# P V as four 64x64 products side by side instead of one product against a block diagonal, in a fused attention and SwiGLU kernel

## The chip, the cores and the metric

The kernel runs on one core of a Trainium2 chip. TensorE (PE) multiplies matrices: a 128x128 block of weights is loaded, and up to 512 columns of the other operand stream through it into a bank of PSUM, the accumulator memory (eight banks, each 128 partitions by 512 fp32). VectorE (DVE), ScalarE (ACT) and GpSimd (POOL) do elementwise work, and only the first two of these three take part in emptying PSUM here; SyncE (SP) issues DMAs. Each engine works through its own queue in order and waits for others by semaphores. The metric is the device time of one execution in microseconds (us), smaller is better.

## The reference

Linformer attention and then a SwiGLU feed-forward block, for 8 batches, 8 heads, 1024 positions, head size 64, 512 model columns, 1536 hidden columns:

```python
k_proj = einsum('ks,bhsd->bhkd', E, k)            # E, F: 64 x 1024
v_proj = einsum('ks,bhsd->bhkd', F, v)            # 64 x 64 per head
attn = softmax(q @ k_proj.T / sqrt(64))           # 1024 x 64 per head
attn_out = attn @ v_proj                          # "P V", 1024 x 64 per head
x = attn_out, heads side by side                  # 8192 x 512
out = (silu(x @ w_gate) * (x @ w_val)) @ w_out    # 8192 x 512
```

In P V both the contraction (64 projected positions) and the output (64 columns of a head) are half as wide as TensorE's array.

## The kernel before

The output rows are done in 16 chunks of 512, two for each batch. The main loop runs over 192 iterations t = 12 c + f: chunk c, block f of 128 hidden columns. Each iteration has four products for the gate (`f_g`, bank tag gps, line 462), four for the value (`f_v`, bank tag vps, line 462), and one or two steps of the down projection of the chunk before (`f_m`, line 564, seven steps for each of two row pairs, in banks y and z, also called yps). ACT takes a tanh of the gate (line 474); DVE multiplies (lines 481, 486). The down projection forms half its products from sums of quarters, hs, made by POOL and DVE (line 547), and its results leave through ACT, DVE and POOL (lines 581 to 600).

The attention of the next batch is spread between these products. The order is written out by hand: every iteration has two slots, 2t after `f_g` and 2t+1 at its end, `put(slot, function, ...)` places a step in a slot, and `place(b)` does so for batch b, with slots counted from s0 = 48 (b - 1). Within a slot loads come first, then steps in the order of their `put`. Nothing is rearranged afterwards. The steps of a batch b are:

- loads of k, v and q from POOL's queue (`load_k`, `load_v`, `load_q`);
- `u_KV`: the k and v projections of all heads, in pairs of products of 64 array columns each; ACT copies k out to ks, DVE copies v out into the block diagonal BDV;
- `u_KT`: k transposed by TensorE, and copied by DVE in four pieces into the block diagonal BD (lines 275, 276);
- `u_TD`, `u_AD`: q and the normalized scores transposed by DMAs from SP's queue, into qTd and AT (bufs=2 each);
- `u_S`, `u_R`, `u_N`: scores of four heads for 256 rows (four products, exp on ACT), sums and reciprocals on DVE, the multiply on POOL into AAd; eight of each for a batch;
- `u_PV`: P V. A pair of heads has its two 64x64 blocks of v on the diagonal of a 128x128 weight block, BDV, whose other two blocks are zero; one product of 512 columns gives both heads of the pair (line 410), and a copy on ACT (line 150) takes it from a bank to xT, which `f_g` and `f_v` read. A chunk has four such products, in four slots.

The pool ps_a has two banks ("a"); g and v have two, y and z one each. Batch 0 and batch 1 have their own arrangements; batch 0's P V runs through `u_PV`, `u_PV2` and `u_PV1`.

Of the kernel before, what the change touches and what calls it, by code (L numbers as in the profile page):

```python
# [16 lines left out]
H = 8  # L17
S = 1024
D = 64
# [19 lines left out]
def kernel(  # L39
# [38 lines left out]
    ident_bf = const.tile([P, P], BF16, name="ident_bf")  # L78
    ident_fp = fw.tile([P, P], FP32, name="ident_fp", tag="th")
    BD = [const.tile([P, H, P], BF16, name=f"BD{i}") for i in range(2)]  # L80
    BDV = [const.tile([P, NPAIR, P], BF16, name=f"BDV{i}") for i in range(2)]
    ks = [const.tile([P, H, D], BF16, name=f"ks{i}") for i in range(2)]
    ksp = [const.tile([P, NPAIR, D], BF16, name=f"ksp{i}") for i in range(2)]
    ET = const.tile([P, NJ, KP], BF16, name="ET")
# [57 lines left out]
    def bank(where, shape, dt, name):  # L142
        if where == "a" and ring["wide"]:
            where = "aaz"[ring["n"] % 3]
            ring["n"] += 1
        pool, tag = banks[where]
        return pool.tile(shape, dt, name=name, tag=tag)
# [4 lines left out]
    def u_KV(b, what="kv", hs=(0, H), at="a"):  # L152

        key = (b, what)
        if key not in kvp:
            kvp[key] = bank(at, [P, H, D], FP32, "kvp")
        t = kvp[key]
        h0, h1 = hs
        todo = [x for x in (("k", 0, ET, kb), ("v", 64, FT, vb)) if x[0] in what]
        for j in range(NJ):  # L160
            for _, lo, w, src in todo:
                nc.tensor.matmul(  # L162
                    out=t[lo : lo + 64, h0:h1].rearrange("p h d -> p (h d)"),
                    lhsT=w[:, j, :],
                    rhs=src[b][:, h0:h1, j, :],
                    start=(j == 0),
                    stop=(j == NJ - 1),
                )
        if "k" in what:
            nc.scalar.copy(out=ks[b % 2][0:64, h0:h1], in_=t[0:64, h0:h1])  # L170
        if "v" in what:
            tv = t[64:128].rearrange("p (a c) d -> p a c d", c=2)
            ps = slice(h0 // 2, h1 // 2)
            nc.vector.tensor_copy(out=BDV[b % 2][0:64, ps, 0:64], in_=tv[:, ps, 0, :])
            nc.vector.tensor_copy(out=BDV[b % 2][64:128, ps, 64:128], in_=tv[:, ps, 1, :])
        if h1 == H:
            kvp.pop(key)

# [15 lines left out]

    def u_V1(b, at="a"):

        t = bank(at, [P, NPAIR, D], FP32, "kvp")
        src = vb[b][:].rearrange("p (a c) j d -> p a c j d", c=2)
        for j in range(NJ):
            for c in range(2):  # L200
                nc.tensor.matmul(
                    out=t[64 * c : 64 * c + 64],
                    lhsT=FT[:, j, :],
                    rhs=src[:, :, c, j, :],
                    start=(j == 0),
                    stop=(j == NJ - 1),
                )
        for c in range(2):
            rows = slice(64 * c, 64 * c + 64)
            nc.vector.tensor_copy(out=BDV[b % 2][rows, :, rows], in_=t[rows])  # L210

    def u_V0(p0, p1, at):

        t = bank(at, [P, p1 - p0, P], FP32, "kvp")
        nc.tensor.matmul(
            out=t[:].rearrange("p a d -> p (a d)"),
            lhsT=zeros[:, 0:P], rhs=zeros[:, 0 : (p1 - p0) * P],
            start=True, stop=False,
        )
        src = vb[0][:].rearrange("p (a c) j d -> p a c j d", c=2)  # L220
        for j in range(NJ):
            for c in range(2):
                nc.tensor.matmul(
                    out=t[64 * c : 64 * c + 64, :, 64 * c : 64 * c + 64],
                    lhsT=FT[:, j, :],
                    rhs=src[:, p0:p1, c, j, :],
                    start=False,
                    stop=(j == NJ - 1),
                )
        nc.scalar.copy(out=BDV[0][:, p0:p1, :], in_=t[:])  # L230

    def u_V0w(p0, p1, at):

        t = bank(at, [P, p1 - p0, 2, D], FP32, "kvp")
        for j in range(NJ):
            nc.tensor.matmul(
                out=t[64:P].rearrange("p a c d -> p (a c) d"),
                lhsT=FT[:, j, :],
                rhs=vb[0][:, 2 * p0 : 2 * p1, j, :],
                start=(j == 0),  # L240
                stop=(j == NJ - 1),
            )
        for c in range(2):
            rows = slice(64 * c, 64 * c + 64)
            nc.scalar.copy(out=BDV[0][rows, p0:p1, rows], in_=t[64:P, :, c, :])

    def turn_ksp(t, b, g):
        nc.tensor.matmul(
# [95 lines left out]
    def u_S(b, u, at="a"):  # L344
        ch, w = divmod(u, 4)
        g, i = divmod(w, 2)
        ps = bank(at, [P, 4, P], FP32, "sc")
        if (b, ch) in BY_DMA:
            t = qT[b, ch, "d"][:].rearrange("p (h i) t -> p i h t", i=2)[:, i, 4 * g : 4 * g + 4]
        else:  # L350
            t = qT.pop((b, u))
        for n in range(4):
            nc.tensor.matmul(  # L353
                out=ps[:, n, :], lhsT=t[:, n, :], rhs=BD[b % 2][:, 4 * g + n, :], start=True, stop=True
            )
        e = aw.tile([P, 4, 2, KP], FP32, name="ee", tag="ee", bufs=4)
        nc.scalar.activation(  # L357
            out=e[:].rearrange("p h j k -> p (h j k)"),
            in_=ps[:].rearrange("p a k -> p (a k)"),
            func=AF.Exp,  # L360
            scale=scale,
        )
        ee[b, u] = e
# [42 lines left out]
    def u_PV(b, ch, pr, eng=nc.scalar):  # L406
        if (b, ch) not in xT:
            xT[b, ch] = x_pool.tile([P, NPAIR, CW], BF16, name="xT", tag=f"xT{ch}")
        ps = bank("a", [P, CW], FP32, "pv")
        nc.tensor.matmul(  # L410
            out=ps[:].rearrange("p (j t) -> p j t", t=P),
            lhsT=BDV[b % 2][:, pr, :],
            rhs=AT[b, ch][:, :, pr, :],
            start=True,
            stop=True,
        )
        copy(eng, xT[b, ch][:, pr, :], ps[:])

    def u_PV2(b, ch, g, i, eng):

        if (b, ch) not in xT:
            xT[b, ch] = x_pool.tile([P, NPAIR, CW], BF16, name="xT", tag=f"xT{ch}")
        ps = bank("a", [P, 2, CW // 2], FP32, "pv")
        for n in range(2):
            nc.tensor.matmul(
                out=ps[:, n].rearrange("p (j t) -> p j t", t=P),
                lhsT=BDV[b % 2][:, 2 * g + n, :],
                rhs=AT[b, ch][:, 2 * i : 2 * i + 2, 2 * g + n, :],
                start=True,
                stop=True,  # L430
            )
        copy(eng, xT[b, ch][:, 2 * g : 2 * g + 2, 256 * i : 256 * (i + 1)], ps[:])

    def u_PV1(b, ch, pr, i, eng):

        ps = bank("a", [P, CW // 2], FP32, "pv")
        nc.tensor.matmul(
            out=ps[:].rearrange("p (j t) -> p j t", t=P),
            lhsT=BDV[b % 2][:, pr, :],
            rhs=AT[b, ch][:, 2 * i : 2 * i + 2, pr, :],  # L440
            start=True,
            stop=True,
        )
        copy(eng, xT[b, ch][:, pr, 256 * i : 256 * (i + 1)], ps[:])
# [211 lines left out]
    def put(s, fn, *a):  # L656
        slots[s].append((fn, a))

    def place(b):
        s0 = 48 * (b - 1)  # L660
        if b == 1:
            put(22, u_TD, 1, 0)
            put(29, u_K1, 1)
            put(32, u_KT, 1)
            put(40, u_V1, 1)
            sa = (35, 36, 37, 38, 41, 42, 43, 44)
            put(41, u_AD, 1, 0)
            put(30, u_TD, 1, 1)
            put(47, u_AD, 1, 1)
            sp = (44, 45, 46, 46, 66, 67, 68, 69)  # L670
        else:
            put(s0 + (10 if b == 2 else 0), u_KV, b)
            put(s0 + (13 if b == 2 else 3), u_KT, b)
            o = 17 if b == 2 else 6
            put(s0 + (9 if b == 2 else -6), u_TD, b, 0)
            put(s0 + (11 if b == 2 else -4), u_TD, b, 1)
            sa = [s0 + o + 3 * j for j in range(NJ)]
            put(sa[3] + 4, u_AD, b, 0)
            put(sa[7] + 4, u_AD, b, 1)
            sp = [s0 + i for i in ((41, 43, 45, 46) if b == 2 else (39, 41, 43, 45)) + (57, 59, 61, 63)]  # L680
        for j in range(NJ):
            put(sa[j], u_S, b, j)
            put(sa[j] + 1, u_R, b, j)
            put(sa[j] + 1, u_N, b, j)
        for i in range(8):
            put(sp[i], u_PV, b, i // 4, i % 4)

    def run_slot(s):
        for fn, a in slots.pop(s, ()):
# [2 lines left out]
    with tc.manual_schedule():  # L692
# [17 lines left out]
        make_identity(nc, ident_fp[:])  # L710
        make_identity(nc, ident_bf[:])
        nc.vector.memset(ks[0][64:P], 0.0)
        nc.vector.memset(BDV[0][:, 0:2], 0.0)

        def turn(which, at, halves=(0, 1), eng=nc.scalar):
            for half in halves:
# [79 lines left out]
        f_mm(0, 1, 1, 0)  # L796
        nc.vector.memset(ks[1][64:P], 0.0)
        nc.vector.memset(BD[1][:], 0.0)
        nc.vector.memset(BDV[1][:], 0.0)
        load_w_gv(5, 7)  # L800
        load_w_gv(7, 8)
        load_q(0, 1, hs=(0, 4))
# [95 lines left out]
```

## Time and profile before

| | |
|---|---|
| time, median of 3 runs | 551.76 us (551.55 to 552.42) |
| the profiled execution's own time | 551.3 us |
| its span, first to last instruction | 549.5 us |
| ACT busy with copies pv to xT, 128x512 | 35.7 us, 61 of 588 ns |
| PE busy with P V, line 410 | 22.4 us, 60 of 379 ns |
| PE busy with the k and v projections, line 162, 512 columns | 11.5 and 11.5 us, 48 of 382 ns each |
| POOL's multiply, line 383, into AAd | 58.4 us, 56 of 1043 ns |

A row of the profile gives start and duration in us, engine, line of the kernel, operation, output<-inputs, and the shapes. A matmul's duration runs from its start to the modelled end of its results; the next one starts before that end, so what a matmul takes of TensorE is the time from its start to the next start. PEld is the loading of weights. Some matmul records are missing from a trace.

### The profile page before, as it was taken

What the parts mean: (1) busy time and instruction counts of PE and PEld (TensorE: products, weight loads), DVE (VectorE), ACT (ScalarE), POOL (GpSimd) and SP (SyncE); (2) the same over time, 40 slices, a digit from 0 to 9 for tenths busy, and PEclk for the clock granted to TensorE, in tenths of its full rate; (3) what the DMA queues carried; (4) which work ended last, traced back from release to release, by engine and by line L of the source; (5) the groups of instructions that cost most, each with busy time, mean ns of one, the idle gap of its engine ahead of it and who ended that gap; (6) DMA issues with size and microseconds to landing.
All of it is one profiled execution on the core that took longest, in us unless ns stands there. A gap on an engine that the chain in (4) does not pass through costs nothing.

```text
span 549.5 us, 9272 instructions
## 1 busy us (share of the span) xinstructions
PE 536.9 (98%) x3438; PEld 317.4 (58%) x3500; DVE 414.5 (75%) x699; ACT 233.3 (42%) x416; POOL 294.6 (54%) x364
## 2 busy tenths in 40 slices
PE   7999999999999999999999999999999999999996
PEld 4654445566556555665555655566556565555565
DVE  3787897788597866978578785788859787676784
ACT  3664453444445433443435434344244533443331
POOL 6851494466627843386534855268461763526162
PEclk9999999999999999999999999999999999999999
DMA  9999989919963698029941399214990213110013
GB/s 205 192 197 188 162 150 178 179 39 140 197 124 78 116 197 149 10 69 159 195 106 39 76 163 197 66 39 93 178 211 18 72 46 76 39 40 17 23 39 116
DMA packets 111630, 62.87 MB, mean 114 GB/s; under 512 B 65888, under 2 KB 102752, under 8 KB 111584
## 3 DMA queue, kind: packets, MB, share of 16 engines
q0 software_dynamic: 43952, 29.49, 38.0%
q1 hardware_dynamic: 66800, 31.20, 26.4%
q10 hardware_dynamic: 832, 1.57, 0.9%
q8 instruction: 27, 0.44, 0.3%
q14 instruction: 19, 0.16, 0.1%
HBM read 60.29 MB, written 16.78 MB: 140 GB/s over the span
## 4 chain that ended last, share of the span: by engine, by line
PE 77%; DVE 10%; DMA 8%; issue 2%; POOL 2%; ACT 1%; DVEq 0%; POOLq 0%; ACTq 0%
PE gps L462 24%; PE vps L462 24%; PE yps L564 22%; DMA qTd<-qb 3%; DVE hs L547 2%; DVE s L481 2%; PE kvp L162 2%; DMA qb<-in_q_dram 2%; PE pv L410 2%; DVE hT L486 2%; PE sc L353 2%; DMA Fraw<-in_F_dram 1%; PE yps L498 1%; DMA wv<-in_moe_w_val_dram 1%; DVE BD L276 1%
## 5 line engine op out<-in xcount | busy, mean ns | idle before, releaser
L462 PE MATMUL vps<-xT,wv 128*128 128x512 bf16 (+1 forms) x761 | 195.0, 377 | 1.7 <-issue 0.8
L462 PE MATMUL gps<-xT,wg 128*128 128x512 bf16 (+1 forms) x727 | 191.0, 377 | 2.1
L474 ACT ACTIVATE th<-gps 128x512 f32<-128x512 f32 x191 | 114.1, 598 | 165.3 <-PE gps L462 149.4
L481 DVE SCALAR_TENSOR_TENSOR s<-th,gps 128x512 f32<-128x512 f32 x191 | 129.3, 677 | 66.3 <-ACT th L474 64.9
L547 POOL TENSOR_TENSOR hs<-hT 128x256 bf16<-128x256 bf16 x180 | 120.5, 691 | 58.9 <-DVE hT L486 58.1
L486 DVE SCALAR_TENSOR_TENSOR hT<-s,vps 128x512 bf16<-128x512 f32 x192 | 132.1, 688 | 20.4 <-PE gps L462 0.5
L462 PEld LDWEIGHTS <-wv 128*128 128x128 bf16 x776 | 73.8, 98 | 83.5 <-issue 3.0
L564 PEld LDWEIGHTS <-hs 128*128 128x128 bf16 x900 | 88.0, 98 | 35.7 <-issue 2.2
L462 PEld LDWEIGHTS <-wg 128*128 128x128 bf16 x776 | 73.9, 98 | 56.2 <-issue 0.6
L383 POOL TENSOR_TENSOR AAd<-ee,rr 128x512 bf16<-128x512 f32 x56 | 58.4, 1043 | 55.8 <-issue 33.7
L594 POOL TENSOR_TENSOR tt<-tt,ysb 128x512 f32<-128x512 f32 x28 | 35.5, 1267 | 68.2 <-DVE tt L593 68.2
L564 PE MATMUL yps<-ws,hs 128*128 128x256 bf16 x540 | 68.6, 272 | 0.4 <-DVE ysb L631 0.2
L583 POOL TENSOR_TENSOR tt<-xs 128x256 f32<-128x256 f32 x30 | 29.4, 982 | 52.2 <-ACT xs L581 52.1
L150 ACT CAST xT<-pv 128x512 bf16<-128x512 f32 (+1 forms) x63 | 36.4, 581 | 45.3 <-PE pv L410 44.2
L368 DVE TENSOR_REDUCE zz<-ee 128x8 f32<-128x512 f32 x64 | 43.3, 677 | 11.1 <-ACT ee L357 11.0
L564 PE MATMUL yps<-ws,hT 128*128 128x256 bf16 x360 | 48.8, 273 | 0.0
L564 PE MATMUL yps<-wo,hs 128*128 128x256 bf16 x360 | 48.6, 273 | 0.1
L547 DVE TENSOR_TENSOR hs<-hT 128x1536 bf16<-128x1536 bf16 (+1 forms) x49 | 46.1, 946 | 0.1
L357 ACT ACTIVATE ee<-sc 128x512 f32<-128x512 f32 x64 | 38.1, 598 | 18.2 <-PE sc L353 18.1
L564 PEld LDWEIGHTS <-hT 128*128 128x128 bf16 x360 | 35.2, 98 | 16.0
L581 ACT COPY xs<-yps 128x512 f32<-128x512 f32 x30 | 17.6, 585 | 30.4 <-PE yps L564 30.3
L588 ACT COPY ysb<-yps 128x512 f32<-128x512 f32 x30 | 17.6, 586 | 24.9 <-PE yps L564 21.6
(99 smaller groups left out, 318.0 us busy)
## 6 DMA issues: line engine op xcount, KB each, us to landing
out_dram<-ysb SPq DMA_DIRECT2D x28, 512.0 KB, 2.7
qb<-in_q_dram POOLq DMA_DIRECT2D x14, 512.0 KB, 19.2
kb<-in_k_dram POOLq DMA_DIRECT2D x7, 1024.0 KB, 10.0
vb<-in_v_dram POOLq DMA_DIRECT2D x7, 1024.0 KB, 14.8
wo<-in_moe_w_out_dram POOLq DMA_DIRECT2D x2, 768.0 KB, 21.5
out_dram<-ysb SPq DMA_DIRECT2D x6, 256.0 KB, 2.3
kraw<-in_k_dram ACTq DMA_DIRECT2D x2, 512.0 KB, 4.8
qb<-in_q_dram POOLq DMA_DIRECT2D x4, 256.0 KB, 7.8
```

The costliest lines, as they stand in the source:

```text
L150: (nc.scalar.copy if eng is nc.scalar else eng.tensor_copy)(out=out, in_=in_)
L357: nc.scalar.activation(out=e[:].rearrange("p h j k -> p (h j k)"), in_=ps[:].rearrange("p a k -> p (a k)"), func=AF.Exp, scale=scale,)
L368: nc.vector.reduce_sum(out=z[:], in_=e[:], axis=AX.X)
L383: eng.tensor_tensor(out=a.rearrange("p j h k -> p h j k"), in0=ee.pop((b, u))[:], in1=rr.pop((b, u))[:].unsqueeze(3).to_broadcast([P, 4, 2 ...
L462: nc.tensor.matmul(out=ps[:, ts], lhsT=(wg, wv)[w][:, kt, f * P : (f + 1) * P], rhs=x[:, kt, ts], start=(kt == 0), stop=(kt == NKT - 1),)
L474: nc.scalar.activation(out=th[:], in_=ps[:], func=AF.Tanh, scale=0.5)
L481: nc.vector.scalar_tensor_tensor(out=s1[:], in0=th[:], scalar=1.0, in1=g[:], op0=ALU.add, op1=ALU.mult)
L486: nc.vector.scalar_tensor_tensor(out=hT[c][:, f, :], in0=s1[:], scalar=0.5, in1=ps[:], op0=ALU.mult, op1=ALU.mult)
L547: eng.tensor_tensor(out=hs[c, m][:, fs, :], in0=quarter(hT[c], *a)[:, fs], in1=quarter(hT[c], *b)[:, fs], op=op,)
L564: nc.tensor.matmul(out=ps, lhsT=lhsT, rhs=ws[m][:, f, :] if rhs is None else rhs, start=(start and f == 0), stop=(f == HF - 1), skip_group ...
L583: nc.gpsimd.tensor_tensor(out=t[:, 0], in0=xs[:, 0], in1=xs[:, 1], op=ALU.add)
L594: nc.gpsimd.tensor_tensor(out=t[:], in0=t[:], in1=yo[c, p][:, 1:3], op=ALU.subtract)
```

## The change

Each head's v block is now a 64x64 weight block of its own. The tile VS holds, in partitions 64 r to 64 r + 63, column block 2 g + e, the block of head 4 g + 2 r + e. `u_PVt` does two heads with rows 0 to 63 of the array into one bank and two with rows 64 to 127 into another; of each two, one writes partitions 0 to 63 and one 64 to 127. The scores of the four heads of a group are stored in the order 0, 2, 1, 3, so that the transposed scores AT lie in the partitions that this needs. All four products of the two groups of a chunk stand in one slot, with four banks (two of a, y and z), and four copies on ACT follow one another, the last first. Batch 0 keeps the block diagonal, and batch 1's first half has its two groups in two slots.

The slots move as well. From the fourth batch on (b = 3) the k and v projection goes from slot s0 to s0 + 8, into a vps bank; `u_KT` from s0 + 3 to s0 + 11, the scores from s0 + 6 + 3 j to s0 + 14 + 3 j, and with them the score transposes. P V is at s0 + 44 and s0 + 56; s0 + 56 is the slot of the next batch's projection, which then comes directly after it.

```diff
-    BDV = [const.tile([P, NPAIR, P], BF16, name=f"BDV{i}") for i in range(2)]
+    BDV = const.tile([P, NPAIR, P], BF16, name="BDV")
+    VS = [const.tile([P, 4, D], BF16, name=f"VS{i}") for i in range(2)]
...
         if "v" in what:
-            tv = t[64:128].rearrange("p (a c) d -> p a c d", c=2)
-            ps = slice(h0 // 2, h1 // 2)
-            nc.vector.tensor_copy(out=BDV[b % 2][0:64, ps, 0:64], in_=tv[:, ps, 0, :])
-            nc.vector.tensor_copy(out=BDV[b % 2][64:128, ps, 64:128], in_=tv[:, ps, 1, :])
+            tv = t[64:128].rearrange("p (g r e) d -> p g r e d", r=2, e=2)
+            for r in range(2):
+                vs = VS[b % 2][64 * r : 64 * r + 64].rearrange("p (g e) d -> p g e d", e=2)
+                nc.vector.tensor_copy(out=vs, in_=tv[:, :, r])
...
-        for c in range(2):
-            rows = slice(64 * c, 64 * c + 64)
-            nc.vector.tensor_copy(out=BDV[b % 2][rows, :, rows], in_=t[rows])
+        nc.vector.tensor_copy(out=VS[b % 2][:], in_=t[:])
...
         for n in range(4):
+            slot = (0, 2, 1, 3)[n] if (b, ch) in BY_DMA else n
             nc.tensor.matmul(
-                out=ps[:, n, :], lhsT=t[:, n, :], rhs=BD[b % 2][:, 4 * g + n, :], start=True, stop=True
+                out=ps[:, slot, :], lhsT=t[:, n, :], rhs=BD[b % 2][:, 4 * g + n, :], start=True, stop=True
             )
...
+    def u_PVt(b, ch, gs, ats):
+        if (b, ch) not in xT:
+            xT[b, ch] = x_pool.tile([P, NPAIR, CW], BF16, name="xT", tag=f"xT{ch}")
+        todo = []
+        for g in gs:
+            ps = [bank(at, [P, CW], FP32, "pv") for at in ats[g]]
+            for r in range(2):
+                rows = slice(64 * r, 64 * r + 64)
+                for e in range(2):
+                    nc.tensor.matmul(
+                        out=ps[r][64 * e : 64 * e + 64].rearrange("p (j t) -> p j t", t=P),
+                        lhsT=VS[b % 2][rows, 2 * g + e, :],
+                        rhs=AT[b, ch][rows, :, 2 * g + e, :],
+                        start=True,
+                        stop=True,
+                    )
+            todo += [(2 * g + r, ps[r]) for r in range(2)]
+        for kt, ps in reversed(todo):
+            nc.scalar.copy(out=xT[b, ch][:, kt, :], in_=ps[:])
...
-            sp = (44, 45, 46, 46, 66, 67, 68, 69)
+            put(45, u_PVt, 1, 0, (0,), ("aa", "aa"))
+            put(46, u_PVt, 1, 0, (1,), ("aa", "aa"))
         else:
-            put(s0 + (10 if b == 2 else 0), u_KV, b)
-            put(s0 + (13 if b == 2 else 3), u_KT, b)
-            o = 17 if b == 2 else 6
+            if b == 2:
+                put(s0 + 10, u_KV, b)
+            else:
+                put(s0 + 8, u_KV, b, "kv", (0, H), "v")
+            put(s0 + (13 if b == 2 else 11), u_KT, b)
             put(s0 + (9 if b == 2 else -6), u_TD, b, 0)
             put(s0 + (11 if b == 2 else -4), u_TD, b, 1)
-            sa = [s0 + o + 3 * j for j in range(NJ)]
+            sa = [s0 + j for j in ((17, 22, 24, 27, 30, 33, 36, 39) if b == 2 else (14, 17, 20, 23, 26, 29, 32, 35))]
             put(sa[3] + 4, u_AD, b, 0)
             put(sa[7] + 4, u_AD, b, 1)
-            sp = [s0 + i for i in ((41, 43, 45, 46) if b == 2 else (39, 41, 43, 45)) + (57, 59, 61, 63)]
+            put(s0 + 44, u_PVt, b, 0, (0, 1), ("aa", "yz"))
...
-        for i in range(8):
-            put(sp[i], u_PV, b, i // 4, i % 4)
+        put(s0 + (68 if b == 1 else 56), u_PVt, b, 1, (0, 1), ("aa", "yz"))
...
-        nc.vector.memset(BDV[1][:], 0.0)
```

More of the change, by code (lines that the diff above doesn't have):

```diff
@@ L195, in u_V1 @@
     def u_V1(b, at="a"):
-        t = bank(at, [P, NPAIR, D], FP32, "kvp")
-        src = vb[b][:].rearrange("p (a c) j d -> p a c j d", c=2)
+        t = bank(at, [P, 4, D], FP32, "kvp")
+        src = vb[b][:].rearrange("p (g r e) j d -> p g r e j d", r=2, e=2)
         for j in range(NJ):
-            for c in range(2):
+            for r in range(2):
                 nc.tensor.matmul(
-                    out=t[64 * c : 64 * c + 64],
+                    out=t[64 * r : 64 * r + 64].rearrange("p (g e) d -> p g e d", e=2),
                     lhsT=FT[:, j, :],
-                    rhs=src[:, :, c, j, :],
+                    rhs=src[:, :, r, :, j, :],
                     start=(j == 0),
@@ L207, in u_V1 @@
                 )
-        for c in range(2):
-            rows = slice(64 * c, 64 * c + 64)
-            nc.vector.tensor_copy(out=BDV[b % 2][rows, :, rows], in_=t[rows])
+        nc.vector.tensor_copy(out=VS[b % 2][:], in_=t[:])
     def u_V0(p0, p1, at):
@@ L229, in u_V0 @@
                 )
-        nc.scalar.copy(out=BDV[0][:, p0:p1, :], in_=t[:])
+        nc.scalar.copy(out=BDV[:, p0:p1, :], in_=t[:])
     def u_V0w(p0, p1, at):
@@ L244, in u_V0w @@
             rows = slice(64 * c, 64 * c + 64)
-            nc.scalar.copy(out=BDV[0][rows, p0:p1, rows], in_=t[64:P, :, c, :])
+            nc.scalar.copy(out=BDV[rows, p0:p1, rows], in_=t[64:P, :, c, :])
     def turn_ksp(t, b, g):
@@ L411, in u_PV @@
             out=ps[:].rearrange("p (j t) -> p j t", t=P),
-            lhsT=BDV[b % 2][:, pr, :],
+            lhsT=BDV[:, pr, :],
             rhs=AT[b, ch][:, :, pr, :],
@@ L417, in u_PV @@
         copy(eng, xT[b, ch][:, pr, :], ps[:])
+    def u_PVt(b, ch, gs, ats):
[4 more added lines that the diff above has]
+            ps = [bank(at, [P, CW], FP32, "pv") for at in ats[g]]
+            for r in range(2):
+                rows = slice(64 * r, 64 * r + 64)
[10 more added lines that the diff above has]
+            nc.scalar.copy(out=xT[b, ch][:, kt, :], in_=ps[:])
     def u_PV2(b, ch, g, i, eng):
@@ L426, in u_PV2 @@
                 out=ps[:, n].rearrange("p (j t) -> p j t", t=P),
-                lhsT=BDV[b % 2][:, 2 * g + n, :],
+                lhsT=BDV[:, 2 * g + n, :],
                 rhs=AT[b, ch][:, 2 * i : 2 * i + 2, 2 * g + n, :],
@@ L438, in u_PV1 @@
             out=ps[:].rearrange("p (j t) -> p j t", t=P),
-            lhsT=BDV[b % 2][:, pr, :],
+            lhsT=BDV[:, pr, :],
             rhs=AT[b, ch][:, 2 * i : 2 * i + 2, pr, :],
@@ L712 @@
         nc.vector.memset(ks[0][64:P], 0.0)
-        nc.vector.memset(BDV[0][:, 0:2], 0.0)
+        nc.vector.memset(BDV[:, 0:2], 0.0)
         def turn(which, at, halves=(0, 1), eng=nc.scalar):
```

## The prediction, made before the changed kernel ran

> **What bounds the kernel now.** I read the engine totals first, then what TensorE waited for, then TensorE's instructions in order of time around the work that changes.
>
> Engine totals and clock (the page), PE being TensorE:
>
> ```profile
> PE 536.9 (98%) x3438; PEld 317.4 (58%) x3500; DVE 414.5 (75%) x699; ACT 233.3 (42%) x416; POOL 294.6 (54%) x364
> PEclk9999999999999999999999999999999999999999
> ```
>
> TensorE is busy 98% at full clock. A busy share can hide small gaps, because a matmul's span (379 ns) is longer than its turn, so I also took start to start: between 45 us and the end of the main loop a 512-column matmul follows the last one after 0.216 us, a 256-column one after 0.109 us. The list of what TensorE waited for holds 1.2, 0.9, 0.8, 0.7 us and less in all: the 0.8 is five times 0.16 behind the k and v projection (below), the rest is start and end. So a TensorE microsecond taken out of the loop is a microsecond of the kernel, and each new TensorE wait counts in full.
>
> TensorE in order of time, first the k and v projection of the sixth batch (index b = 5), then products P V of that batch's first half (start, duration, line, output<-inputs):
>
> ```profile
> 343.48 1.03 PE L462 MATMUL gps<-xT,wg 128*128 128x512 bf16 x4
> 344.44 0.40 PE L162 MATMUL kvp<-kb,ET 128*64 128x512 bf16 x1
> 344.44 0.40 PE L162 MATMUL kvp<-vb,FT 128*64 128x512 bf16 x1
> 344.68 0.38 PE L162 MATMUL kvp<-kb,ET 128*64 128x512 bf16 x1
> 344.68 0.38 PE L162 MATMUL kvp<-vb,FT 128*64 128x512 bf16 x1
> ...
> 345.98 0.38 PE L162 MATMUL kvp<-kb,ET 128*64 128x512 bf16 x1
> 345.98 0.38 PE L162 MATMUL kvp<-vb,FT 128*64 128x512 bf16 x1
> 346.52 0.81 PE L462 MATMUL vps<-xT,wv 128*128 128x512 bf16 x3 [0.16 <-issue]
> 347.16 0.82 PE L564 MATMUL yps<-ws,hT 128*128 128x256 bf16 x6
> ...
> 400.60 0.38 PE L410 MATMUL pv<-AT,BDV 128*128 128x512 bf16 x1
> 400.82 1.03 PE L462 MATMUL gps<-xT,wg 128*128 128x512 bf16 x4
> ```
>
> Two readings. The product at 400.60 takes 0.216 us of TensorE (next start 400.82), though half its weights are the zeros of BDV. And the projection's products, 64 columns of the array each, start in pairs at the same moment: two run side by side for the price of one. Going in and out has a price: gps starts at 343.48 and four turns would end at 344.35, but the pair comes at 344.44 (0.09 late), the second pair follows after 0.24 rather than 0.216 (0.02), and one record of vps is missing, so its first is at 346.52 - 0.216 = 346.30, 0.11 later than 345.98 + 0.216. Check over the whole: 343.48 to 347.16 is 3.68 us for 16 turns of 0.216 (3.46), so 0.22 for one excursion.
>
> Where the scores' transposes land (DMA issues: median us to landing; what waits for P V):
>
> ```profile
> AT<-AAd SPq DMA_TRANSPOSE x14, 9.1
> DMA to landing us min/median/max: 4.2/9.1/16.7
> ```
>
> **The change part by part.** Only batches 1 to 7 are touched, 14 half-batch steps.
>
> *Products.* Removed from each step: 4 turns, 0.864 us. Added: 8 products of 64x64, four side by side, that is two rounds. No row here shows two row halves of the array at work at once with separate results. From below, a round costs one turn as a pair of the projection does (0.216); from above, the row halves run one after the other (0.432 a round). I take 0.216: the nearest row is the pairs, which already read all 128 partitions twice at once, as a round does; new is only that two banks are written at once. Weight loads: 110 ns each for 64 columns in the projection, issued while the pair before runs, so hidden.
>
> On the point without a row the Trainium skill, "TensorE: Matmul & The Clock Gate", Part 3 on packing small matmuls, states that row and column tiles work at once, with some 4 ns more for each further tile. No run here shows it; by it a round is 12 ns longer than a turn, and the sum below would be 2.9 us.
>
> *Excursions.* A step alone: 0.09 + 0.02 + 0.11 = 0.22, as the projection's. So 0.864 - 0.432 - 0.22 = 0.21 saved. Eight such: the first halves of batches 2 to 7, the second halves of 1 and 7: 1.68 us. The first half of batch 1 is split over two places with other work between: two excursions, each 0.432 - 0.216 - 0.22 = 0. Directly ahead of the projection (second halves of batches 2 to 6): the exit is shared, but from 64x64 to 128x64 another change may cost between nothing and an entry (0.11). I take the entry, since both are changes of shape: 0.864 - 0.432 - 0.11 = 0.32 each, 1.60 for five. Sum 3.28 us; 3.83 if that change is free; with row halves in turn, -0.22 x 8 - 0.22 x 2 - 0.11 x 5 = -2.75, a loss.
>
> *Score order.* The swapped slots move results inside a bank; same products, no cost. The v copies on DVE stay two of 64x256 (0.43 us each); batch 1 has one instead of two. Zeroing BDV of odd batches goes (0.27 us of DVE in the start). DVE has no part in the bound there.
>
> *Evacuation.* Four copies pv to xT on ACT stood two slots apart (0.59 us, idle before each); now they come in one burst. Behind one another they start about every 0.55 us (403.44, 403.93, 404.48 for a copy, a copy and a tanh). With T the start of the last gps product before the step: tanh at T+0.41, copies at 0.97, 1.52, 2.07, 2.62, done at 3.2. Who waits: bank z is needed by the down projection's seventh step in the first-half place, at T+0.31 (round 1) +0.24 +0.22 +0.11 (exit) +0.86 = T+1.73; its copy goes first and ends at T+1.56, which covers it by 0.17 us. The next gps wants its tanh from T+3.7 on: later than 3.2. xT is wanted after T+5. In the second-half place ks waits behind the four copies, from T+2.85 to T+3.15; the v copies on DVE wait for ks, end near T+4.6, and free the vps bank that the projection now borrows: the next vps to use it starts at T+5.8. I cost this at nothing; if each burst slips by one more copy (0.55 us), the z bank loses 0.55 - 0.17 = 0.38 in six steps, 2.3 us.
>
> The Trainium skill, "TensorEngine Tiling (Array Packing)", section PSUM Bottleneck, speaks against the change: tiling speeds up the products but not the evacuation of PSUM, which then may be the limit. By that rule a step would be as long as its four copies on ACT, and nothing would be saved. This trace differs: ACT is 42% busy, and the next readers come after the copies.
>
> *Moved by eight slots.* From batch 3 on the projection, scores and their transposes start 8 slots later (a slot is 65.57/48 = 1.37 us), k's block copies three slots behind the projection as before. These had 0.05 us to spare: the last BD copy ended at 353.09 + 0.43 = 353.52, the scores started at 353.56. In the new place the DVE item ahead of them is an output sum (0.60 us to the next) instead of an hs sum (0.87), so 0.3 us to spare: nothing.
>
> *SP's queue.* The first half's scores transpose of batches 3 to 6 now issues amid the next batch's loads. Before, at 370.79, it met none and landed in 4.3 us; the second half's at 387.05 met them and landed 15.9 us later. Moved, POOL's multiply ends near 382, landing takes 13.3 to 16.7 us as the contended ones did, so 395 to 399; P V is reached near 403.3 (404.28 less three old products and 0.32). It is covered by 4 us or more; without that cover each microsecond costs four. In batch 2 the second half's transpose now stands behind batch 3's first q transpose, which waited for its q load until 150.70 and held SP 3.5 us. From above: issue at 154.2, landing 4.2 to 5.8 us later, 158.4 to 160.0, against a need at 157.9 (160.05 less the projection's 1.95 and 0.2): up to 2.1 us, once. From below nothing: without that transpose's packets in the way (2080 of 31 ns over 16 engines, 4 us) the q load lands near 147. I take nothing, since the packets it shared with do move behind it. POOL's loads keep their slots, and the multiplies move past them by one place at most.
>
> **Sum.** The profiled execution took 551.3 us (span 549.5 plus 1.8 around it), 0.46 under the median 551.76. 551.3 - 3.28 = 548.0, or 548.5 against the median. What tells from no change is about 0.2%, 1.1 us.
>
> **The rivals.**
> 1. *Row halves run in turn.* A round takes two turns. For it: no row shows the contrary. Against: pairs share the array freely. Ends slower: 551.76 + 2.75 = 554.5. It decides once a round takes 0.216 + 3.28/28 = 0.33 us (28 rounds).
> 2. *Excursions cost twice as much* with 64x64 tiles: 0.22 more in each of ten alone, 0.11 in each of five ahead of the projection, 2.75 us of the gain: 551.2, no change. For it: shape changes drain the array, and four tiles are loaded instead of two. Against: the projection's first round is late by a time that does not look like a load each (0.09 with two loads of 0.11).
> 3. *A wait in its place*: the scores transpose of batches 3 to 6 lands after P V is reached. From 4.3 + 0.8 us of lateness on, four stalls of 0.8 us eat the gain: 551.8. For it: every contended transpose took 13 us or more. Against: the longest took 16.7.
>
> **How the numbers follow.** Forecast 0.71 (548.5, own range 547.5 to 550.2: free change of shape 548.0 less the 0.4 us spread of the runs; 550.2 with some 1.7 of z bank or batch 2 stall). Rival 1 0.13, rival 2 0.10, rival 3 0.06. The range reaches over 2 and 3 to 552.0 and leaves out rival 1. Faster: 0.68 of the forecast and 0.05 of the partial forms of 2 and 3; slower: rival 1 and 0.02 of the worse forms of 3; same: the rest, 0.12.
>
> **What would show it.** Right: products of 64x512 starting four at a time within some 10 ns, the next four 0.216 to 0.24 later; 0.09 and 0.11 at the ends; a batch's period 65.57 - 0.53 = 65.0 us; no new wait of TensorE. Wrong: second pair of a group a full turn behind the first (rival 1), longer gaps at the ends (2), TensorE idle for the scores transpose ahead of P V (3), or gaps ahead of the seventh down-projection step (z bank).

## The result and the profile after

The changed kernel takes 548.53 us (median of 6 runs, 547.95 to 548.67), the kernel before 552.34 us beside it (6 runs, 551.55 to 553.61): a ratio of 0.9934, interval 0.9924 to 0.9945, faster by 0.66%. Forecast were 548.5 us and a range of 547.5 to 552.0. The two profiled executions stand 3.13 us apart in span, 549.53 and 546.40 us (in time 551.3 and 548.17), and the ledger below is made of these two.

The page of the changed kernel, engine totals and clock, answers to the first fence of the prediction:

```profile
PE 534.6 (98%) x3494; PEld 313.6 (57%) x3556; DVE 412.5 (75%) x697; ACT 233.2 (43%) x416; POOL 294.6 (54%) x364
PEclk9999999999999999999999999999999999999999
```

TensorE is still the bound, at full clock, with 2.3 us less of busy time. TensorE in order of time (start, duration, line, output<-inputs): a first-half step, and a second-half step with the projection behind it:

```profile
401.29 1.03 PE L484 MATMUL gps<-xT,wg 128*128 128x512 bf16 x4
402.25 0.63 PE L430 MATMUL pv<-AT,VS 64*64 64x512 bf16 x8
402.80 0.82 PE L484 MATMUL vps<-xT,wv 128*128 128x512 bf16 x2
...
416.90 1.03 PE L484 MATMUL gps<-xT,wg 128*128 128x512 bf16 x4
417.85 0.63 PE L430 MATMUL pv<-AT,VS 64*64 64x512 bf16 x8
418.41 0.40 PE L163 MATMUL kvp<-kb,ET 128*64 128x512 bf16 x1
418.41 0.40 PE L163 MATMUL kvp<-vb,FT 128*64 128x512 bf16 x1
```

Eight products of 64x512 take the place of four of 128x512. In the trace their starts are 3, 3 and 4 ns apart, then 230 ns, then 3, 3 and 4 ns again: four side by side, two rounds. The Trainium skill, "TensorE: Matmul & The Clock Gate", Part 3 on packing small matmuls, gives about 4 ns for each further tile; this trace agrees. From the last gps start (401.94) to the step is 309 ns rather than 216, and from the step's last start to the next product 308 ns. So a step alone lasts 309 + 10 + 230 + 10 + 308 = 867 ns where four products and the one ahead took 5 x 216 = 1080: 213 ns saved, of which the second product behind gives back 10 (226 ns instead of 216). Ahead of the projection the way on takes 306 ns, so a change from 64x64 to 128x64 costs as much as any other.

Busy time of the engines in whole batches, from one projection to the next (the stretch and its length in us, then busy time and count of PE, PEld, DVE, ACT and POOL, clock, DMA share, GB/s); before:

```profile
213.36:278.94 65.58, 65.00 (x415) 38.64 (x424) 50.45 (x85) 27.89 (x49) 35.99 (x45) 1.00 0.63 114
278.94:344.51 65.57, 65.00 (x414) 38.64 (x424) 50.43 (x85) 27.90 (x49) 35.95 (x45) 1.00 0.64 112
```

and after:

```profile
223.84:288.70 64.86, 64.44 (x425) 38.07 (x429) 50.15 (x85) 27.93 (x50) 35.94 (x44) 1.00 0.65 114
288.70:353.55 64.85, 64.43 (x424) 38.08 (x428) 50.13 (x85) 27.91 (x50) 35.93 (x44) 1.00 0.67 114
```

A batch is 0.71 us shorter; forecast was 0.53. And the list of what TensorE waited for has a new entry after the change, the first scores transpose of batch 2, which no rival had priced (rival 3 named those of batches 3 to 6):

```profile
PE pv L430 <- DMA AT<-AAd: 1.0, 1, 1.0
```

**The ledger**, from the two traces. Whole steps alone: 8 x 0.203 = 1.62 us gained. Steps ahead of the projection: 1173 ns before (four products and the projection's entry) against 865, 5 x 0.308 = 1.54 gained. The split step of batch 1: 0.32 lost. A wait of TensorE that was there before and is gone: 5 x 0.21 = 1.05 gained. The new wait: 1396 - 309 ns = 1.09 lost. Together 2.80 gained in the loop. The end is 0.54 us shorter (below), the start of this execution 0.20 longer (the tanh of the twenty-first iteration starts at 67.70 instead of 67.50 us): 2.80 + 0.54 - 0.20 = 3.14, against 3.13 between the spans.

### The profile page after: what moved, and what is told of

It is laid out like the page before. It is cut to its first block, busy times and chain, and to the rows that moved or that the text cites. A ratio compares the mean times of both kernels' runs of the same rounds, so it can differ in the third digit from the quotient of the medians.

```text
span 546.4 us, 9372 instructions
## 1 busy us (share of the span) xinstructions
PE 534.6 (98%) x3494; PEld 313.6 (57%) x3556; DVE 412.5 (75%) x697; ACT 233.2 (43%) x416; POOL 294.6 (54%) x364
## 4 chain that ended last, share of the span: by engine, by line
PE 84%; DMA 12%; POOL 2%; issue 1%; ACT 0%; DVE 0%; POOLq 0%; DVEq 0%; ACTq 0%
PE vps L484 26%; PE gps L484 26%; PE yps L586 24%; DMA qTd<-qb 3%; DMA AT<-AAd 3%; PE sc L353 2%; DMA qb<-in_q_dram 2%; PE kvp L163 2%; PE pv L430 2%; DMA Fraw<-in_F_dram 1%; PE yps L520 1%; DMA wv<-in_moe_w_val_dram 1%; POOL wv L127 0%; POOL AA L383 0%; POOL wg L127 0%
## 5 line engine op out<-in xcount | busy, mean ns | idle before, releaser
L439 ACT CAST xT<-pv 128x512 bf16<-128x512 f32 x56 | 28.9, 601 | 2.3 <-PE pv L430 2.3
## 6 DMA issues: line engine op xcount, KB each, us to landing
qb<-in_q_dram POOLq DMA_DIRECT2D x14, 512.0 KB, 18.6
```

What stands on the lines that cost most here:

```text
L439: nc.scalar.copy(out=xT[b, ch][:, kt, :], in_=ps[:])
```

## The experiments

The theory: the four-way products are the gain, at 0.2 us a step alone and 0.3 ahead of the projection; the moved slots give and take about one microsecond each. The rival: the moved slots, which relieve DVE, are the gain.

**New products in the old slots.**

```diff
-            if b == 2:
-                put(s0 + 10, u_KV, b)
-            else:
-                put(s0 + 8, u_KV, b, "kv", (0, H), "v")
-            put(s0 + (13 if b == 2 else 11), u_KT, b)
+            put(s0 + (10 if b == 2 else 0), u_KV, b)
+            put(s0 + (13 if b == 2 else 3), u_KT, b)
+            o = 17 if b == 2 else 6
...
+            sa = [s0 + o + 3 * j for j in range(NJ)]
```

> The four 64x64 products as in the changed kernel, but projection, scores and transposes in the slots of the kernel before (projection at s0, scores from s0 + 6), P V at s0 + 44 and s0 + 56. Theory (the gain is the products'): thirteen whole steps alone, each 0.864 to 0.655 us, so 0.2 x 13 = 2.6 us below the kernel before; TensorE's wait of 0.21 us for DVE's sum L593 in five batches stays as before, and the wait of 1.0 us for batch 2's scores transpose does not appear. Rival (the gain comes from the moved slots): within 1 us of the kernel before.

Measured: 550.06 us against 551.75, ratio 0.9970 (0.9959 to 0.9981), 1.7 us gained. A batch takes 64.96 us, 0.61 less than before. Two misses in the working. First, a wait that was not forecast: the scores of batch 2 share slot 68 with batch 1's second half, and need a bank that the burst of copies still holds. TensorE in order of time in this kernel:

```profile
109.79 0.63 PE L430 MATMUL pv<-AT,VS 64*64 64x512 bf16 x8
112.09 0.38 PE L353 MATMUL sc<-BD,qTd 128*128 128x128 bf16 x4 [1.67 <-ACT xT L439]
```

It cost 1.73 us (the way on takes 2.04 us rather than 0.31); the changed kernel has batch 2's scores in slots 22 and 24 instead of 20 and 23, and does not wait here. Second, the wait for DVE's sum was expected to stay, and it went: 13 x 0.203 + 1.05 - 1.73 - 0.32 = 1.64, what was measured. So the products alone do give their part, and the wait went without the scores being moved.

**Old products in the new slots.** BDV is doubled and filled as before, the score order is the old one, and the burst of copies stays:

```diff
-            for r in range(2):
-                rows = slice(64 * r, 64 * r + 64)
-                for e in range(2):
-                    nc.tensor.matmul(
-                        out=ps[r][64 * e : 64 * e + 64].rearrange("p (j t) -> p j t", t=P),
-                        lhsT=VS[b % 2][rows, 2 * g + e, :],
-                        rhs=AT[b, ch][rows, :, 2 * g + e, :],
+            for r in range(2):
+                nc.tensor.matmul(
+                    out=ps[r][:].rearrange("p (j t) -> p j t", t=P),
+                    lhsT=BDVs[b % 2][:, 2 * g + r, :],
+                    rhs=AT[b, ch][:, :, 2 * g + r, :],
```

> The slots of the changed kernel and its burst of four copies, but each step is four products against the block diagonal again, with the scores in their old order. Theory: products as dear as before (0.864 a step); the moved slots give back five waits of 0.21 us (-1.05) and bring the wait for batch 2's scores transpose (+0.9), so within 0.5 us of the kernel before. Rival (the moved slots are the gain): about 3 us below the kernel before.

Measured: 551.50 us against 551.75, ratio 0.9994 (0.9986 to 1.0003), no difference that can be told. A batch takes 65.36 us, 0.21 less than before, and TensorE waits 1.00 us for batch 2's transpose. The rival falls: the slots alone gain nothing in sum. The two traces add up: 1.05 us gained by the five waits and 0.54 at the end, 1.00 lost at the transpose, 0.25 in batch 1's split step, and 0.09 in the start, 0.25 us in sum; the spans are 549.53 and 549.27.

**The vanished wait.** Before the change, TensorE and DVE in order of time, at the seventh down-projection step of the first row pair, early in a batch's first half:

```profile
359.64 1.03 PE L462 MATMUL vps<-xT,wv 128*128 128x512 bf16 x4
360.71 0.49 PE L564 MATMUL yps<-ws,hs 128*128 128x256 bf16 x3
```

```profile
358.90 0.64 DVE L481 SCALAR_TENSOR_TENSOR s<-th,gps 128x512 f32<-128x512 f32 x1
359.64 0.69 DVE L486 SCALAR_TENSOR_TENSOR hT<-s,vps 128x512 bf16<-128x512 f32 x1
360.25 0.41 DVE L593 TENSOR_TENSOR tt<-tt,yps 128x256 f32<-128x256 f32 x1
```

Four vps products from 359.64 are over at 360.50, all four are recorded, and the step starts at 360.71: a wait of 0.21 us, for the sum L593, which reads the half bank that the step adds to and ends at 360.66. It comes in five batches. The waits list shows nothing of it, because the matmul's modelled end (0.38 us after its start) covers all but 0.04. DVE is a whole iteration behind there (its product hT of 359.64 starts when the next value products only begin), after the projection's copies, the four BD copies and the three hs sums.

The first try moved one product of the kernel before by a slot:

```diff
-...(39, 41, 43, 45)) + (57, 59, 61, 63)]
+...(39, 41, 43, 45)) + (56, 59, 61, 63)]
```

> The kernel before with one thing changed: the first product P V of each second half (batches 2 to 7) stands in slot s0 + 56 instead of s0 + 57, so that 0.216 us of TensorE's work comes ahead of the down-projection step that waits 0.21 us for DVE's sum L593. Theory (that wait was removed by work placed ahead of it, not by moving the scores): the five waits go, a batch takes 65.36 instead of 65.57 us, 1.0 us below the kernel before. Rival (the moved scores removed it): the wait stays and the time is that of the kernel before.

Measured: 551.74 us against 551.68, ratio 1.0003 (0.9994 to 1.0012); 65.57 us a batch, and the wait stays. It tells nothing of the cause: slot 57 stands ahead of the waiting step too, so no work was put in front. The second product, from slot 59, does cross the step:

```diff
-...(39, 41, 43, 45)) + (57, 59, 61, 63)]
+...(39, 41, 43, 45)) + (57, 58, 61, 63)]
```

> The kernel before with its second product P V of each second half (batches 2 to 7) in slot s0 + 58 instead of s0 + 59. The experiment with slot 56 moved a product that stood ahead of the waiting down-projection step in either place, so it put nothing more in front; this one moves 0.216 us of TensorE's work from behind that step to ahead of it. Theory (TensorE runs into DVE's backlog there, and any work put ahead fills the wait of 0.21 us): the five waits shrink to nearly nothing, a batch takes 65.36 instead of 65.57 us, 1.0 us below the kernel before. Rival (the moved scores or the burst of copies removed it): the wait stays, 65.57 us.

Measured: 550.65 us against 551.69, ratio 0.9982 (0.9973 to 0.9992), 1.0 us gained; 65.36 us a batch. In this kernel, TensorE and then DVE:

```profile
359.18 0.38 PE L410 MATMUL pv<-AT,BDV 128*128 128x512 bf16 x1
359.39 1.03 PE L462 MATMUL vps<-xT,wv 128*128 128x512 bf16 x4
360.26 0.82 PE L564 MATMUL yps<-ws,hs 128*128 128x256 bf16 x6
```

```profile
359.79 0.41 DVE L593 TENSOR_TENSOR tt<-tt,yps 128x256 f32<-128x256 f32 x1
```

The sum ends at 360.20 and the step starts at 360.26, right behind the last vps product. So in the kernel before one product in another slot was worth 1.0 us. In the changed kernel and in both kernels above the whole second-half step stands ahead of that place, and none of the three has the wait; that the step fills it in the changed kernel, rather than the moved copies and sums of DVE, was not taken apart.

**The new wait.** SP in order of time in the changed kernel:

```profile
124.19 8.70 SPq L337 DMA_TRANSPOSE AT<-AAd  x1
133.00 0.72 SPq L622 DMA_DIRECT2D out_dram<-ysb  x1
145.16 2.96 SPq L330 DMA_TRANSPOSE qTd<-qb  x1
148.21 3.03 SPq L337 DMA_TRANSPOSE AT<-AAd  x1
```

Batch 2's first scores transpose, issued at 124.19, landed at 142.78, 18.6 us later; P V was reached at 141.74. The load of k for batch 3 was issued at 122.15, two microseconds ahead of the transpose. Before, it was issued at 123.22, and the transpose right behind it at 123.30: landed in 13.3 us. The experiment puts the loads of batch 3 two slots later:

```diff
-        s0 = 48 * (b - 1) - (20 if b == 3 else 24)
+        s0 = 48 * (b - 1) - (18 if b == 3 else 24)
```

> The changed kernel with batch 3's four loads two slots (2.7 us) later. Theory: batch 2's first scores transpose is late because those loads run ahead of it; it lands in 9 us or less of contention instead of 18.6, TensorE's wait of 1.0 us before P V at 142.8 us goes, and the kernel is 1.0 us faster than the changed one, some 4.5 us below the kernel before. Rival: the wait is only handed on (to the second scores transpose or to batch 3's projection), and the time stays as the changed kernel's.

Measured: 547.21 us against 551.75, ratio 0.9918 (0.9904 to 0.9931), 4.5 us gained, about 0.9 more than the changed kernel (by the two ratios; the intervals overlap). The span is 545.4 us, 1.03 less than the changed kernel's. The transpose was issued at 123.72, with the load at 123.63, and landed after 12.4 us rather than the 9 expected. SP, then TensorE:

```profile
123.72 2.51 SPq L337 DMA_TRANSPOSE AT<-AAd  x1
```

```profile
140.84 1.03 PE L484 MATMUL gps<-xT,wg 128*128 128x512 bf16 x4
141.79 0.63 PE L430 MATMUL pv<-AT,VS 64*64 64x512 bf16 x8
142.35 0.82 PE L484 MATMUL vps<-xT,wv 128*128 128x512 bf16 x3
```

No wait ahead of P V, and none elsewhere in its place; the second transpose lands at 156.04, and its products start at 157.40. This is the fastest of the kernels run.

**The bank that was covered by 0.17 us.** The down-projection step that needs bank z behind a first-half step is the fifth of the second row pair (`f_m` takes bank z at n = 4, counted from 0); the prediction and the expectation below call it the seventh. In the changed kernel, ACT and then TensorE:

```profile
402.92 2.06 ACT L439 CAST xT<-pv 128x512 bf16<-128x512 f32 x4
```

```profile
403.68 1.47 PE L586 MATMUL yps<-ws,hs 128*128 128x256 bf16 x12
```

```diff
-        for kt, ps in reversed(todo):
-            nc.scalar.copy(out=xT[b, ch][:, kt, :], in_=ps[:])
+        for n, (kt, ps) in enumerate(reversed(todo)):
+            for _ in range(2 if n == 0 and len(gs) == 2 and ch == 0 else 1):
+                nc.scalar.copy(out=xT[b, ch][:, kt, :], in_=ps[:])
```

> The changed kernel with the first copy of each first-half burst (bank z, batches 2 to 7) done twice: 0.55 us more of ACT in front of the others. Theory (the prediction's timing, z bank covered by 0.17 us): TensorE waits 0.38 us ahead of the seventh down-projection step in six batches, 2.3 us slower than the changed kernel. Rival (evacuation has ample room): no difference. Rival of the page on tiling (evacuation is already the limit): 6 x 0.55 = 3.3 us slower.

Measured: 551.42 us against 551.75, ratio 0.9989 (0.9981 to 0.9998), so 3.0 us slower than the changed kernel by the ratios. TensorE in order of time, in the kernel with the doubled copy:

```profile
404.83 1.04 PE L485 MATMUL vps<-xT,wv 128*128 128x512 bf16 x4
406.20 1.47 PE L587 MATMUL yps<-ws,hs 128*128 128x256 bf16 x12 [0.34 <-ACT xT L440]
```

The step starts at 406.20 instead of 405.70: 0.50 us in each of six batches, 3.0 us. The extra copy took 0.62 us of ACT and not 0.55: it starts 0.03 us after the end of the first, which has the same target, while copies to different targets follow one another after 0.48 us, ahead of the end of the one before. And the cover was 0.12 us and not 0.17: in the changed kernel the copy that frees bank z ends at 403.51, the step here started 0.05 us after such an end (406.15 and 406.20), and TensorE got there at 403.68. So the burst is off TensorE's path in the changed kernel, by 0.12 us. That the full price of a copy (6 x 0.62 = 3.7) is not paid, and that the changed kernel has no wait at this place, speaks against evacuation as its limit; but the distance is small.

**Evacuation by two engines**, on top of the later loads:

```diff
-        for kt, ps in reversed(todo):
-            nc.scalar.copy(out=xT[b, ch][:, kt, :], in_=ps[:])
+        for n, (kt, ps) in enumerate(reversed(todo)):
+            copy(nc.scalar if n % 2 == 0 else nc.vector, xT[b, ch][:, kt, :], ps[:])
```

> The kernel with the later loads, with the second and fourth copy of each burst on DVE instead of ACT. Theory (evacuation does not lie on TensorE's path): no gain, within 0.5 us of the kernel with the later loads, slower if DVE's 0.69 us copies push its sums back. Rival (the page on tiling: both engines are needed to keep up): faster by up to 14 x 0.5 us.

Measured: 549.15 us against 551.68, ratio 0.9955 (0.9943 to 0.9968), 1.9 us slower than the kernel with the later loads by the medians, 2.0 by the ratios. A batch takes 64.86 us, the same to 0.01. Of the 1.92 us between the two spans 1.59 are one wait, in batch 1's split step, where the second pair's bank is now freed by DVE behind its other work (the two pairs start 1.89 us apart instead of 0.30); the other 0.33 us lie ahead of the loop's twenty-first iteration. TensorE in order of time:

```profile
79.05 0.40 PE L430 MATMUL pv<-AT,VS 64*64 64x512 bf16 x2
80.94 0.40 PE L430 MATMUL pv<-AT,VS 64*64 64x512 bf16 x2 [1.49 <-DVE xT L151]
```

The section PSUM Bottleneck of the Trainium skill's "TensorEngine Tiling (Array Packing)", which asks for both engines, finds nothing to mend here: the copies of a burst were not what a batch waited for.

**The place ahead of the projection.**

```diff
-                put(s0 + 8, u_KV, b, "kv", (0, H), "v")
+                put(s0 + 9, u_KV, b, "kv", (0, H), "v")
```

> The changed kernel with the k and v projection of batches 3 to 7 one slot later, so that a value product and a down-projection step lie between P V and it. Theory (a change of shape costs some 0.09 to 0.11 us, and side by side one is saved): each of the five pays one change more, 0.11 x 5 = 0.55 us slower than the changed kernel, a batch 64.96 instead of 64.86 us. Rival (nothing is shared, the place is worth nothing): 64.86 us as before.

Measured: 548.71 us against 551.68, ratio 0.9944 (0.9931 to 0.9956); a batch takes 64.96 us in each of four periods, 0.10 more than in the changed kernel. One of them, in the columns used above:

```profile
226.73:291.69 64.96, 64.54 (x421) 38.00 (x428) 50.21 (x84) 27.99 (x49) 35.90 (x44) 1.00 0.64 114
```

By the ratios the difference is 0.55 us, though their intervals overlap; the period settles it. Standing directly ahead of the projection saves one change of shape, 0.1 us a batch, 0.5 us in all.

## Why the prediction was right, point by point

*The bound, and the time of a round.* Right. Every saved piece of TensorE time shows in the batch's period. The second round starts 0.24 us after the first, as the projection's second pair did; the upper bound, row halves in turn, did not occur (rival 1).

*Excursions.* Right to 0.01 us: 0.203 against 0.21 for a step alone, 0.308 against 0.32 ahead of the projection, sum 3.16 against 3.28 us. The changes of shape cost what the projection's cost, also between two narrow shapes. Rival 2 falls by the same rows.

*The split step of batch 1.* Wrong, 0 forecast, 0.32 lost. In its second half the two row halves start 300 ns apart (3, 300, 3): with two banks of "a" and z in turn, one of the pair's banks still waits for a copy of the group before: those copies end at 78.91, and the second row half starts at 78.97. The old products in the new slots wait there too, 0.25 us. The term took two rounds for granted and did not ask when the banks come free.

*"The list of what TensorE waited for holds ... the rest is start and end."* Wrong: there were five waits of 0.21 us in the loop. A gap of 423 ns between starts looks like two turns of 216 with a missing record between; but all four records of that group were there. Counting the records of a group would have told. The forecast thus left out a gain of 1.05 us.

*"It is covered by 4 us or more"*, and transposes of 13.3 to 16.7 us. The mechanism was right and the size off: transposes issued amid the loads took 18.5 to 19.7 us, and the first halves of batches 3 to 6 landed 2.8, 1.6, 2.4 and 2.6 us ahead of their products. The one that came late was the first half of batch 2, which the text did not work out at all; it looked at batch 2's second half, which landed 5 us early (153.07, first product 158.43), and the q load that the q transpose ahead of it waited for landed at 145.09, not at 150.65 as before. Over all fourteen scores transposes of the changed kernel, where the prediction's row had 4.2/9.1/16.7:

```profile
DMA to landing us min/median/max: 4.3/13.7/19.7
```

Rival 3 named the right kind of wait and the wrong batches: 1.09 us, once.

*Evacuation at nothing.* Right: no wait for it in the changed kernel's loop, outside batch 1's split step; a copy follows another after 0.48 us rather than 0.55 (the two copies that the prediction names, at 403.44 and 403.93, stand 0.49 apart), and the cover of bank z was 0.12 rather than 0.17 us.

*The sum.* In the loop 2.80 us against 3.28, because two omissions of about a microsecond cancel and the split step loses 0.32. With the shorter end the profiled executions differ by 3.13. That the medians differ by 3.8 us comes in part from the runs of the kernel before, which spread by 2 us here: in the sets of the experiments it had medians of 551.68 to 551.75, 3.2 us above the changed kernel's. The ratio's interval, 3.0 to 4.2 us, holds the ledger. The forecast time was met to 0.03 us by such luck, not by working to that precision.

## What to carry to other kernels

Where TensorE's starts have no gaps, the half of an array that multiplies zeros is real time, and four 64x64 products side by side get it back, less one entry and one exit (0.22 us here) for each place where they stand: put narrow products next to each other. Look for hidden waits by start to start and by counting the records of each group, since here five waits of 0.21 us, hidden behind a matmul's recorded span of 0.38 us, appeared in no list; such a wait may be filled by moving one independent product ahead of it (1.0 us here, with no other change). When a step is moved, write down for every batch which transfers its inputs now share the queues with, the odd ones first: every loss that was not forecast sat in the batches with an arrangement of their own.

## What the runs showed of the hardware that was not expected

A DMA transpose issued 2.0 us behind a 1 MB load took 18.6 us to land, and 12.4 to 13.5 us in three kernels that issue it less than 0.1 us behind it, while its issue held SP for 8.7 us in the one case and 2.5 to 2.6 us in the others. What in the queues makes the difference was not taken apart.

The end of the kernel, from the last matmul's end to the end of the span, took 3.83 to 3.85 us in the six kernels with the moved slots and 4.39 to 4.42 us in the four without, whichever products they used: the last output landed 2.13 instead of 2.68 us after its issue, though nothing at the end was changed. This is 0.54 us of the gain; its cause stays open.
